# A retention layer and a feed-forward layer in one kernel: two small products swapped, the scores of two chunks in one place, one more block by seven products

## The chip, the cores and the metric

The kernel runs on one core of a Trainium2 chip. The metric is the device time of one execution in microseconds (us); the median of three executions is given. The kernel is written in Bass with its own instruction order: the order in which the Python code issues an operation is the order in which its engine runs it (`tc.manual_schedule()`), and each engine waits, in that order, for the semaphores of what it reads and of the buffers that it overwrites.

## The reference

```python
gamma = 1.0 - 2.0 ** (-5.0 - np.arange(H))            # H = 8 heads
for t in range(S):                                    # S = 768 tokens, 4 sequences
    state = gamma * state + outer(k[t], v[t])         # 64 x 64 for each head
    y[t] = scale * q[t] @ state
x = y, heads side by side                             # 3072 tokens x 512
h = x @ w_in                                          # 512 -> 2048
g = h * tanh(log1p(exp(h)))                           # mish
out = g @ w_out                                       # 2048 -> 512, float32
```

## The kernel before

**Chunks and blocks.** The 3072 tokens are 24 chunks of 128, six to a sequence. `BLOCKS` puts them into 11 blocks: block 0 of four chunks, blocks 1 to 10 of two chunks (256 tokens). For each chunk the recurrence is done by products: `scores` (8 products of 64 rows by 128 columns, one for each head, into a PSUM tile `at`), `mask` (VectorE multiplies them with a triangle, giving `am`), `outer` (key by value into `u_ps`), `state` (VectorE adds the last state into `su`, then `su` times the decay gives `st`, on VectorE or, in the blocks by seven products, on GpSimd), and `y_two` (`past` from the state, `present` from `am`), whose result ScalarE copies out as `xt`. All this is done one block ahead: while block b goes through the feed-forward layer, the scores, masks and y of block b+1 lie between its matmuls. GpSimd casts and scales q, k and v (`casts`, three operations a chunk), and SyncE's queue turns them by a transposing DMA (`next_chunk`).

**Plain blocks.** A block of 256 tokens has 64 matmuls of 256 columns for the first product (`g1`, L475), a mish on ScalarE after each eight, and 32 matmuls of 512 columns for the second (`g2_mm`, L497). Its other work is placed by `plan_of`, a table from step to work.

**Blocks by seven products.** From block `SEVEN` on, `g1_seven` and `seven` use the scheme of Strassen and Winograd: a product of 2 by 2 blocks from seven products of half the size, not eight. In `g1_seven` the hidden features are four slices of 512; slices 0 and 2 are made together by seven products of 8 matmuls with 128 columns (L599), slices 1 and 3 are plain (`plain`, L623: 8 matmuls of 256 columns each, two for a slice). In `seven` the whole second product is made by seven products of 8 matmuls with 256 columns (L688). The operands are sums of blocks:
- `wsum` (`win_sums`) and `tmat` (`weight_sums`) are sums of the weights, made once, on VectorE;
- `xsum` (`x_sums`) and `gsum` (`sums_a` for s1 and s2 in two halves, `sums_b` for s3, `sums_c` for s4) are sums of a block's x and g, made for each block, on VectorE.

Three PSUM tiles `pb`, `px`, `pe` accumulate several products; between two of them the running value is copied out (`snap`, ScalarE: `m1`, `m5`, `u2`) and added later on VectorE (`plus`, giving `c11`, `c12`, `c22`). So a product that goes on accumulating in `px` waits until the copy or the sum that reads `px` is done. `mish_of` then makes g from each quarter. Half 0 of `gsum`'s s2 reads g of slices 0 and 2, half 1 reads slices 1 and 3, thus the mish of `plain(3, 1)`, the last of the first product. The second product begins with a(0,0), a(0,1), then s2 with t2: its matmuls 0 to 3 read half 0, matmuls 4 to 7 half 1.

**Where the other work lies in such a block.** `steps_of` is a table from a place's name to work: `p2` (outer, first state), `p6`, `p7` (second state, `sums_a` half 0), `p4` (first chunk's scores and mask), `end` (`sums_a` half 1, second chunk's scores, the next casts), and in `seven` `m2` (second mask), `m7` (`y_two`), `m3` (`x_sums`).

**The weight sums.** `win_sums` runs in block 1 (`blk + 2 == SEVEN`), `weight_sums` in block 2 (`blk + 1 == SEVEN`), one item after each step of the block's loop. Their tiles come from pools that they share with the staging buffers of the weights (`wt`) and the g tiles of block 0 (`g0`).

Of the kernel before, what the change touches and what calls it, by code (L numbers as in the profile page):

```python
# [9 lines left out]
FP16 = mybir.dt.float16  # L10
FP32 = mybir.dt.float32
AF = mybir.ActivationFunctionType
ALU = mybir.AluOpType
# [3 lines left out]
def kernel(  # L17
# [12 lines left out]
    P = 128  # L30
# [4 lines left out]
    TB = 512  # L35
# [5 lines left out]
    NFB = d_ff // P  # L41
    NBP = d_model // P
# [22 lines left out]
    wstage = ctx.enter_context(tc.tile_pool(name="rn_wstage", bufs=3))  # L65
    gp = ctx.enter_context(tc.tile_pool(name="rn_g", bufs=2))
# [29 lines left out]
    for c in range(2):  # L96
        t = tri_first[c * HB:(c + 1) * HB]
# [17 lines left out]
    gtiles, tmats, gsums = {}, [], []  # L115
    wsums, hsnaps, tsums = [], [], {}
    nsnap = [0]
    SEVEN = 3
    nload, ncast = [0], [0]
    stores = []  # L120

# [389 lines left out]
    def weight_sums(half):  # L511
        n, hf = NFB // 2, d_model // 2
        if half == 0:
            tmats.extend(
                wstage.tile([P, 2, n, hf], FP16, name="tmat", tag="wt", bufs=4)
                for _ in range(2))
            gsums.extend(
                wstage.tile([P, 4, n, P], FP16, name="gsum", tag="wt", bufs=4)
                for _ in range(2))
        f = slice(half * FPS, (half + 1) * FPS)  # L520
        t1, t2 = tmats[0][:, 0, f], tmats[0][:, 1, f]
        t3, t4 = tmats[1][:, 0, f], tmats[1][:, 1, f]
        b11, b12 = wouts[half][:, :, :hf], wouts[half][:, :, hf:]
        b21, b22 = wouts[half + 2][:, :, :hf], wouts[half + 2][:, :, hf:]
        sub = ALU.subtract
        return [
            lambda: nc.vector.tensor_tensor(t1, b12, b11, op=sub),
            lambda: nc.vector.tensor_tensor(t2, b22, t1, op=sub),
            lambda: nc.vector.tensor_tensor(t3, b22, b12, op=sub),
            lambda: nc.vector.tensor_tensor(t4, b21, t2, op=sub),  # L530
        ]
# [12 lines left out]
        nc.vector.tensor_tensor(s2, s1, a11, op=ALU.subtract)  # L544

    def win_sums():
        wsums.append(gp.tile([P, 4, NBP // 2, TB], FP16, name="wsum", tag="g0"))
        hsnaps.append(gp.tile([P, 4, TB], FP32, name="hsnap", tag="g0"))
        sub, n = ALU.subtract, NBP // 2
        todo = []  # L550
        for half in range(2):
            s1, s2, s3, s4 = [
                wsums[0][:, i, :, half * (TB // 2):(half + 1) * (TB // 2)] for i in range(4)]
            a11, a12 = wins[0, half][:, :n], wins[0, half][:, n:]
            a21, a22 = wins[2, half][:, :n], wins[2, half][:, n:]
            todo.append([(s1, a21, a22, ALU.add), (s2, s1, a11, sub)])
            todo.append([(s3, a11, a21, sub), (s4, a12, s2, sub)])

        def work(ops):
            for dst, x, y, f in ops:  # L560
                nc.vector.tensor_tensor(dst, x, y, op=f)
        return [lambda ops=ops: work(ops) for ops in todo]
# [14 lines left out]
    def g1_seven(blk, steps):  # L577
        n = NBP // 2
        gt = gtiles[blk, 0] = gp.tile([P, NFB, 2 * P], FP16, name="g", tag="g")
        for fb in range(NFB):  # L580
            gts[blk, fb] = gt[:, fb]
        pb, px, pe = [mmps.tile([P, FPS, P], FP32, name="h_ps", tag="mm") for _ in range(3)]

        def a(i, j):
            return lambda f, d: win(2 * i, f, j * n + d)

        def s(i):
            return lambda f, d: wsums[0][:, i - 1, d, f * P:(f + 1) * P]

        def b(i, j):  # L590
            return lambda d: x_part(blk, i, j)[:, d]

        def t(i):
            return lambda d: tsums[blk][:, i - 1, d]

        def mm(h_ps, w, x, first=False):
            for f in range(FPS):
                for d in range(n):
                    nc.tensor.matmul(  # L599
                        h_ps[:, f], w(f, d), x(d), start=first and f == 0 and d == 0,  # L600
                        stop=d == n - 1, skip_group_check=True)

        def snap(h_ps):
            x = hsnaps[0][:, nsnap[0] % 4].rearrange("p (f t) -> p f t", t=P)
            nsnap[0] += 1
            nc.scalar.copy(x, h_ps)  # L606
            return x

        def mish_of(i, j, h):
            nc.scalar.activation(  # L610
                gt[:, 2 * i * FPS:(2 * i + 1) * FPS, j * P:(j + 1) * P], h, AF.Mish,
                scale=inv_boost3)

        def plus(h_ps, x):
            h = hp.tile([P, FPS, P], FP32, name="hsum", tag="hsum", bufs=3)
            nc.vector.tensor_tensor(h, h_ps, x, op=ALU.add)  # L616
            return h

        def plain(s, half):
            h_ps = mmps.tile([P, 2, 2 * P], FP32, name="h_ps", tag="mm")  # L620
            for j in range(2):
                for bp in range(NBP):
                    nc.tensor.matmul(  # L623
                        h_ps[:, j], win(s, 2 * half + j, bp), xt(blk, bp),
                        start=bp == 0, stop=bp == NBP - 1)
            fb = s * FPS + 2 * half
            nc.scalar.activation(gt[:, fb:fb + 2], h_ps, AF.Mish, scale=inv_boost3)  # L627

        def step(name):
            for fn, *args in steps.get(name, ()):  # L630
                fn(*args)

        mm(px, a(0, 0), b(0, 0), True)
        m1 = snap(px)
        mm(pb, a(0, 1), b(1, 0), True)
        c11 = plus(pb, m1)
        step("p2")
        mm(pe, s(1), t(1), True)
        m5 = snap(pe)
        mm(px, s(2), t(2))  # L640
        u2 = snap(px)
        mish_of(0, 0, c11)
        step("p6")
        plain(1, 0)
        mm(pe, s(4), b(1, 1))
        c12 = plus(pe, u2)
        mm(px, s(3), t(3))
        c22 = plus(px, m5)
        mish_of(0, 1, c12)
        mish_of(1, 1, c22)  # L650
        step("p7")
        plain(1, 1)
        mm(px, a(1, 1), t(4))
        mish_of(1, 0, px)
        step("p4")
        plain(3, 0)
        plain(3, 1)
        step("end")

# [104 lines left out]
    def first_block():  # L764
# [85 lines left out]
            31: [(y_two, 1)],  # L850
        }
        o_tiles = [None] * CPB
        for u in range(2, 2 * NFB):
            if u < NFB:
                g1(0, u)
            elif u < 2 * NFB - 2:
                w = u - NFB
                for t in range(CPB):
                    if w == 0:
                        o_tiles[t] = mmps.tile([P, d_model], FP32, name="o_ps", tag="mm")  # L860
                    g2_mm(o_tiles[t], 0, t, w)
            else:
                for t in range(CPB // 2) if u % 2 == 0 else range(CPB // 2, CPB):
                    for w in range(NFB - 2, NFB):
                        g2_mm(o_tiles[t], 0, t, w)
                    g2_out(o_tiles[t], 0, t, 1)
            for fn, *args in plan.get(u + 1, ()):
                fn(*args)

    def next_chunk(g):  # L870
        if g < NCK:
# [15 lines left out]
    def steps_of(blk):  # L887
        a, nb = first[blk] + 4, blk + 1
        ahead = nb < len(BLOCKS)

        def only(*work):
            return list(work) if ahead else []
        return {
            "p2": only((outer_next, nb), (state_next, nb, 0)),
            "p6": [(cast_to, a + 1), (next_chunk, a), (store_due, 1)],
            "p7": [(store_due, 2), *only((state_next, nb, 1)), (sums_a, blk, 0)],
            "p4": [(store_due, 3), *only((scores, a - 2), (mask, a - 2))],
            "end": [(sums_a, blk, 1), *only((scores, a - 1)),
                    (cast_to, a + 2), (next_chunk, a + 1)],
            "m2": only((mask, a - 1)),  # L900
            "m7": only((y_two, nb)),
            "m3": only((x_sums, nb)),
        }

    def plan_of(blk):
        a = first[blk] + 4
        early, then_seven = blk == 1, blk + 1 == SEVEN
        plan = {1: [(cast_to, a + 1)],
# [8 lines left out]
    for blk in range(1, len(BLOCKS)):  # L917
        if blk >= SEVEN:
            steps = steps_of(blk)
# [5 lines left out]
        extra = []  # L925
        if blk + 1 == SEVEN:
            extra = weight_sums(0) + weight_sums(1)
        if blk + 2 == SEVEN:
            extra = win_sums()
        for u in range(2 * n1):  # L930
            store_due(u)
            if u < n1:
# [1 line left out]
            else:  # L934
                t, part = divmod(u - n1, 4)
# [8 lines left out]
            if extra:  # L944
                extra.pop(0)()
        if blk + 1 == SEVEN:
            x_sums(SEVEN)
    store_due(2 * NFB)
# [30 lines left out]
```

## Time and profile before

| | |
|---|---|
| time, median of 3 (lowest to highest) | 208.18 us (207.81 to 208.47) |
| the profiled execution's own time | 207.9 us |
| its span in the profile | 206.0 us |
| TensorE (PE) busy | 197.2 us |
| VectorE (DVE) busy | 143.1 us |
| ScalarE (ACT) busy | 98.3 us |
| GpSimd (POOL) busy | 90.6 us |
| granted TensorE clock | 1.0 over the span |

The start of each block is the start of its first matmul in the timeline of PE: block 1 at 50.12 us, block 2 at 66.31, block 3 at 82.43, then 97.80, 113.03, 128.49, 143.73, 158.97, 174.43, and block 10 at 189.67. The length of a block is the difference of two such starts. The work of a block depends a little on where a sequence of six chunks begins: of blocks 3 to 9, blocks 5 and 8 have 8 outer and 8 past products, blocks 4 and 7 have 8 and 4, blocks 3, 6 and 9 have 4 and 8; block 2 has 8 and 8, and block 10 has none, and no scores.

A row of the timeline reads: start, time from its first start to its last end, engine, line, operation, output and input, number of instructions, and in brackets the idle time before it with what ended it. A matmul's time in such a row holds its way through the array (219 ns for 128 columns, 273 ns for 256), so the time that a matmul takes of PE is read from the distance of the starts: eight matmuls of 128 columns take 0.45 us, eight of 256 columns 0.87 us.

### The profile page before, as it was taken

What the parts mean: (1) busy time and instruction counts of PE and PEld (TensorE: products, weight loads), DVE (VectorE), ACT (ScalarE), POOL (GpSimd) and SP (SyncE); (2) the same over time, 40 slices, a digit from 0 to 9 for tenths busy, and PEclk for the clock granted to TensorE, in tenths of its full rate; (3) what the DMA queues carried; (4) which work ended last, traced back from release to release, by engine and by line L of the source; (5) the groups of instructions that cost most, each with busy time, mean ns of one, the idle gap of its engine ahead of it and who ended that gap; (6) DMA issues with size and microseconds to landing.
All of it is one profiled execution on the core that took longest, in us unless ns stands there. A gap on an engine that the chain in (4) does not pass through costs nothing.

```text
span 206.0 us, 5180 instructions
## 1 busy us (share of the span) xinstructions
PE 197.2 (96%) x2167; PEld 150.2 (73%) x2167; DVE 143.1 (69%) x234; ACT 98.3 (48%) x171; POOL 90.6 (44%) x83
## 2 busy tenths in 40 slices
PE   6788999999999999999999999999999999999993
PEld 2355444456855865988988988888888888888882
DVE  2796644169937986788897787686897687686542
ACT  2462763242611621653653653753753743843840
POOL 4162000519955760399182594598091693200000
PEclk9999999999999999999999999999999999999999
DMA  5999999998999999939998159959999062200202
GB/s 177 299 316 363 386 387 279 292 220 176 201 247 262 216 221 237 180 70 214 227 253 178 35 109 225 178 105 267 194 256 190 18 156 56 100 0 26 80 28 77
DMA packets 95896, 38.64 MB, mean 188 GB/s; under 512 B 82305, under 2 KB 89985, under 8 KB 95873
## 3 DMA queue, kind: packets, MB, share of 16 engines
q1 hardware_dynamic: 92608, 37.50, 80.3%
q10 hardware_dynamic: 3264, 0.82, 2.4%
q8 instruction: 17, 0.28, 0.5%
q14 instruction: 7, 0.05, 0.1%
HBM read 27.30 MB, written 6.29 MB: 163 GB/s over the span
## 4 chain that ended last, share of the span: by engine, by line
PE 83%; DVE 9%; ACT 2%; DMA 2%; issue 2%; DVEq 0%
PE o_ps L688 24%; PE h_ps L475 13%; PE o_ps L497 11%; PE h_ps L599 11%; PE h_ps L623 11%; DVE hsum L616 5%; PE at L371 3%; PE y_ps L414 2%; DMA qfirst<-in_q_dram 2%; PE y_ps L404 2%; PE u_ps L385 2%; DVE am L377 1%; PE h_ps L760 1%; ACT xt L460 1%; DVE qfirst L196 1%
## 5 line engine op out<-in xcount | busy, mean ns | idle before, releaser
L319 POOL TENSOR_TENSOR qk<-qf,qvs 128x512 f16<-128x512 f32 x20 | 22.5, 1127 | 28.4 <-DMA qf<-in_q_dram 26.4
L623 PE MATMUL h_ps<-xt,win 128*128 128x256 f16 x256 | 31.9, 273 | 0.0
L398 POOL TENSOR_TENSOR st<-su,gcm 128x512 f16<-128x512 f32 x9 | 11.9, 1321 | 41.7 <-DVE su L397 31.3
L497 PE MATMUL o_ps<-wout,g 128*128 128x512 f16 x128 | 30.1, 380 | 0.0
L324 POOL TENSOR_SCALAR qk<-kf 128x512 f16<-128x512 f32 x18 | 27.8, 1546 | 2.1 <-DMA kf<-in_k_dram 0.6
L377 DVE TENSOR_TENSOR am<-at,tri 128x1024 f16<-128x1024 f32 x20 | 24.1, 1214 | 4.6 <-PE at L371 4.6
L688 PEld LDWEIGHTS <-gsum 128*128 128x128 f16 x256 | 24.4, 98 | 3.6 <-DVE gsum L666 0.2
L475 PE MATMUL h_ps<-xt,win 128*128 128x256 f16 (+1 forms) x184 | 26.5, 305 | 0.3
L623 PEld LDWEIGHTS <-win 128*128 128x128 f16 x256 | 23.7, 98 | 3.1
L475 PEld LDWEIGHTS <-win 128*128 128x128 f16 x184 | 18.0, 98 | 9.0 <-issue 0.8
L491 ACT ACTIVATE g<-h_ps 128x512 f16<-128x512 f32 x32 | 19.0, 597 | 11.4 <-PE h_ps L475 10.0
L325 POOL TENSOR_TENSOR v<-vf,qvs 128x512 f16<-128x512 f32 x20 | 21.6, 1079 | 6.3 <-DMA vf<-in_v_dram 4.9
L460 ACT CAST xt<-y_ps 128x1024 f16<-128x1024 f32 x10 | 10.1, 1012 | 28.9 <-PE y_ps L414 21.6
L616 DVE TENSOR_TENSOR hsum<-h_ps,hsnap 128x512 f32<-128x512 f32 x24 | 15.8, 686 | 9.4 <-PE h_ps L599 8.2
L688 PE MATMUL o_ps<-tmat,gsum 128*128 128x256 f16 x192 | 22.3, 273 | 0.0
L627 ACT ACTIVATE g<-h_ps 128x512 f16<-128x512 f32 x32 | 19.0, 593 | 4.8 <-PE h_ps L623 4.8
L497 PEld LDWEIGHTS <-g 128*128 128x128 f16 x128 | 11.7, 98 | 13.0 <-issue 0.3
L606 ACT COPY hsnap<-h_ps 128x512 f32<-128x512 f32 x24 | 13.3, 588 | 15.6 <-PE h_ps L599 15.6
L688 PEld LDWEIGHTS <-g 128*128 128x128 f16 x192 | 18.2, 98 | 2.8
L694 ACT COPY snap<-o_ps 128x256 f32<-128x256 f32 x24 | 8.9, 372 | 20.3 <-PE o_ps L688 20.3
L702 DVE TENSOR_TENSOR osb<-o_ps,snap 128x256 f32<-128x256 f32 x24 | 10.1, 419 | 11.7 <-PE o_ps L688 9.0
L610 ACT ACTIVATE g<-hsum 128x512 f16<-128x512 f32 x24 | 15.0, 635 | 3.4 <-DVE hsum L616 3.4
(94 smaller groups left out, 291.0 us busy)
## 6 DMA issues: line engine op xcount, KB each, us to landing
kf<-in_k_dram SPq DMA_DIRECT2D x23, 256.0 KB, 5.1
vf<-in_v_dram SPq DMA_DIRECT2D x23, 256.0 KB, 5.1
out_dram<-osb SPq DMA_DIRECT2D x22, 256.0 KB, 3.8
qf<-in_q_dram SPq DMA_DIRECT2D x19, 256.0 KB, 4.0
wt<-in_moe_w_out_dram SPq DMA_DIRECT2D x3, 1024.0 KB, 8.9
wi<-in_moe_w_in_dram SPq DMA_DIRECT2D x4, 512.0 KB, 7.3
wi<-in_moe_w_in_dram SPq DMA_DIRECT2D x2, 1024.0 KB, 11.3
qfirst<-in_q_dram SPq DMA_DIRECT2D x2, 512.0 KB, 5.0
```

The source lines that it names most:

```text
L319: nc.gpsimd.tensor_tensor(q16, qf, qs.unsqueeze(2).broadcast_to((P, H, D)), op=ALU.mult)
L324: nc.gpsimd.tensor_scalar(k16, kf, BOOST, None, op0=ALU.mult)
L325: nc.gpsimd.tensor_tensor(v16, vf, vs.unsqueeze(2).broadcast_to((P, H, D)), op=ALU.mult)
L377: nc.vector.tensor_tensor(am, ats.pop(g), tri.unsqueeze(1).unsqueeze(1).broadcast_to((P, 2, HP, C)), op=ALU.mult)
L475: nc.tensor.matmul(h_ps[:, j], win(s, f, bp), xt(blk, bp), start=(bp == 0), stop=(bp == NBP - 1))
L491: nc.scalar.activation(gt, h_ps, AF.Mish, scale=inv_boost3)
L497: nc.tensor.matmul(o_ps, gts[blk, fb][:, t * P:(t + 1) * P], wouts[s][:, f, cols], start=(fb == 0), stop=(fb == NFB - 1))
L599: nc.tensor.matmul(h_ps[:, f], w(f, d), x(d), start=first and f == 0 and d == 0, stop=d == n - 1, skip_group_check=True)
L616: nc.vector.tensor_tensor(h, h_ps, x, op=ALU.add)
L623: nc.tensor.matmul(h_ps[:, j], win(s, 2 * half + j, bp), xt(blk, bp), start=bp == 0, stop=bp == NBP - 1)
L627: nc.scalar.activation(gt[:, fb:fb + 2], h_ps, AF.Mish, scale=inv_boost3)
L688: nc.tensor.matmul(o_ps, x(f), w(f), start=first and f == 0, stop=f == n - 1, skip_group_check=True)
```

## The change

It makes block 2 a block by seven products too (`SEVEN = 2`): `weight_sums` moves from block 2 to block 1, and `win_sums` from block 1 into the second product of block 0, in eight items of one operation each. For that `wsum` and one of the two `gsum` tiles change pools. In `g1_seven`, s3 with t3 (into `px`) and its sum `c22` come ahead of s4 with b(1,1) (into `pe`) and its sum `c12`, and their two mish activations change places with them. The scores of both chunks and the first mask lie in a new place `h2`, between `plain(3, 0)` and `plain(3, 1)`; the second mask stays at `m2`.

```diff
-    SEVEN = 3
+    SEVEN = 2
...
-            gsums.extend(
-                wstage.tile([P, 4, n, P], FP16, name="gsum", tag="wt", bufs=4)
-                for _ in range(2))
+            gsums.append(wstage.tile([P, 4, n, P], FP16, name="gsum", tag="wt", bufs=4))
+            gsums.append(gp.tile([P, 4, n, P], FP16, name="gsum", tag="g0"))
+            hsnaps.append(gp.tile([P, 4, TB], FP32, name="hsnap", tag="g0"))
...
     def win_sums():
-        wsums.append(gp.tile([P, 4, NBP // 2, TB], FP16, name="wsum", tag="g0"))
-        hsnaps.append(gp.tile([P, 4, TB], FP32, name="hsnap", tag="g0"))
+        wsums.append(wstage.tile([P, 4, NBP // 2, TB], FP16, name="wsum", tag="wt", bufs=4))
...
-            todo.append([(s1, a21, a22, ALU.add), (s2, s1, a11, sub)])
-            todo.append([(s3, a11, a21, sub), (s4, a12, s2, sub)])
+            todo.append([(s1, a21, a22, ALU.add)])
+            todo.append([(s2, s1, a11, sub)])
+            todo.append([(s3, a11, a21, sub)])
+            todo.append([(s4, a12, s2, sub)])
...
         plain(1, 0)
+        mm(px, s(3), t(3))
+        c22 = plus(px, m5)
         mm(pe, s(4), b(1, 1))
         c12 = plus(pe, u2)
-        mm(px, s(3), t(3))
-        c22 = plus(px, m5)
+        mish_of(1, 1, c22)
         mish_of(0, 1, c12)
-        mish_of(1, 1, c22)
         step("p7")
         plain(1, 1)
         mm(px, a(1, 1), t(4))
         mish_of(1, 0, px)
         step("p4")
         plain(3, 0)
+        step("h2")
         plain(3, 1)
         step("end")
...
+        extra = []
         for u in range(2, 2 * NFB):
...
+            if u == NFB + 1:
+                extra = win_sums()
+            if extra:
+                extra.pop(0)()
...
-            "p4": [(store_due, 3), *only((scores, a - 2), (mask, a - 2))],
-            "end": [(sums_a, blk, 1), *only((scores, a - 1)),
-                    (cast_to, a + 2), (next_chunk, a + 1)],
+            "p4": [(store_due, 3)],
+            "h2": only((scores, a - 2), (scores, a - 1), (mask, a - 2)),
+            "end": [(sums_a, blk, 1), (cast_to, a + 2), (next_chunk, a + 1)],
...
-        if blk + 2 == SEVEN:
-            extra = win_sums()
```

## The prediction, made before the changed kernel ran

> **What bounds the kernel now.** First the page: engines, then the chain of waits.
>
> ```profile
> PE 197.2 (96%) x2167; PEld 150.2 (73%) x2167; DVE 143.1 (69%) x234; ACT 98.3 (48%) x171; POOL 90.6 (44%) x83
> PE 83%; DVE 9%; ACT 2%; DMA 2%; issue 2%; DVEq 0%
> ```
>
> PE is busy 197.2 of 206.0 us and holds 83% of the chain; the granted clock is 1.0. So what counts is PE's own work and the places where it stands still. For these, PE's timeline of block 4 (97.80 to 113.03), from `plain(1, 0)` to s2 with t2:
>
> ```profile
> 100.03 1.04 PE L623 MATMUL h_ps<-xt,win 128*128 128x256 f16 x8
> 100.90 0.61 PE L599 MATMUL h_ps<-xt,wsum 128*128 128x128 f16 x8
> 101.35 0.61 PE L599 MATMUL h_ps<-xsum,wsum 128*128 128x128 f16 x8
> 101.80 1.04 PE L623 MATMUL h_ps<-xt,win 128*128 128x256 f16 x8
> 102.96 0.61 PE L599 MATMUL h_ps<-xsum,win 128*128 128x128 f16 x8
> 103.50 0.40 PE L371 MATMUL at<-qkt 64*128 64x128 f16 x8
> 103.83 1.92 PE L623 MATMUL h_ps<-xt,win 128*128 128x256 f16 x16
> 105.68 0.40 PE L371 MATMUL at<-qkt 64*128 64x128 f16 x8
> 106.01 1.92 PE L688 MATMUL o_ps<-wout,g 128*128 128x256 f16 x16
> 107.77 2.78 PE L688 MATMUL o_ps<-tmat,gsum 128*128 128x256 f16 x24
> ```
>
> `plain(1, 1)` starts at 101.80 and takes 0.87, to 102.67. The next product, a(1,1) with t4, starts at 102.96: 0.29 us lost. It goes on in `px`, so it waits for `c22`, the second of the two sums in the first row below (from VectorE's timeline; the row after it is ScalarE's, the copies `m5` and `u2`):
>
> ```profile
> 101.62 1.29 DVE L616 TENSOR_TENSOR hsum<-h_ps,hsnap 128x512 f32<-128x512 f32 x2 [0.76 <-PE h_ps L599]
> ...
> 99.84 1.07 ACT L606 COPY hsnap<-h_ps 128x512 f32<-128x512 f32 x2 [0.81 <-PE h_ps L599]
> ```
>
> The sums end at 102.91, and PE goes on 0.05 later. The same wait stands in all eight blocks by seven products.
>
> Second, the scores. The 8 at 103.50 move what follows by more than their row says: from 102.96 to 103.83 are 0.87, of which the product takes 0.45, so 0.42 to 0.43 for the scores; likewise 105.68 (103.83 to 106.01 less 16 x 0.109 = 0.44). In plain block 2 both chunks' scores stand together:
>
> ```profile
> 66.31 7.15 PE L475 MATMUL h_ps<-xt,win 128*128 128x256 f16 x64
> 73.39 0.62 PE L371 MATMUL at<-qkt 64*128 64x128 f16 x16
> 73.95 2.76 PE L497 MATMUL o_ps<-wout,g 128*128 128x512 f16 x12
> ```
>
> 73.95 - 66.31 - 64 x 0.109 = 0.66 us for 16, against 0.87 for twice 8: 0.21 less.
>
> **The change, part by part.**
>
> *The swap.* s3 with t3 now ends 0.45 earlier and `c22` is the first sum. Counted from the block's start in block 4: s3 with t3 runs at 3.10 to 3.55, `c22` starts 0.27 behind it (as the first sum does now: 101.35 to 101.62) and ends 0.69 later, at 4.51; with 0.05, PE may go on at 4.56. But PE is busy with s4 and `plain(1, 1)` until 4.87. The wait is gone, covered by 0.3. A smaller one comes in: s3 with t3 accumulates on U2, so it waits for the copy `u2`, ending at 99.84 + 1.07 = 100.91, plus 0.05, where PE is ready at 100.90. So 0.06 stays. Behind it on PE is all the rest, so it counts in full; the sums and mish behind it move by 0.06 too. Gain 0.29 - 0.06 = 0.23 to 0.24 in each of blocks 3 to 10: 1.9 us.
>
> *The scores in one place.* 0.21 us in each of blocks 3 to 9 (block 10 has none): 1.45 us. The second `at` tile is the one that `u_ps` leaves when the second `su` is done (102.83 + 0.68, at 5.7 in the block; the scores start at 6.2): no wait. The first mask is queued on VectorE between the two halves of `sums_a`; scores end near 6.9 with the way out, and half 0 is done at 6.7 to 7.6 as now, so the mask ends by 8.8, about where it ends now.
>
> *What this uncovers.* `plain(3, 1)` ended at 105.57 (7.77 in the block) and ends at 7.77 again: 0.44 saved ahead of it, 0.43 of scores moved in front of it. The second product now follows at once and not 0.44 later. So s2's matmul 4, the first on half 1 of s2, is due 0.87 + 0.87 + 0.44 = 2.18 behind `plain(3, 1)`, where it had 2.6. Half 1 needs the mish of `plain(3, 1)` (L543 starts 0.84 behind its end) and two operations of VectorE; undisturbed (0.46 + 0.42) they are done at 1.72, disturbed not:
>
> ```profile
> 121.65 0.49 DVE L543 TENSOR_TENSOR gsum<-g 128x512 f16<-128x512 f16 x1 [0.79 <-ACT g L627]
> 122.17 1.15 DVE L544 TENSOR_TENSOR gsum<-gsum,g 128x512 f16<-128x512 f16 x1
> ...
> 182.83 0.42 DVE L543 TENSOR_TENSOR gsum<-g 128x512 f16<-128x512 f16 x1 [0.80 <-ACT g L627]
> 183.29 0.42 DVE L544 TENSOR_TENSOR gsum<-gsum,g 128x512 f16<-128x512 f16 x1
> ...
> 120.59 1.27 POOL L398 TENSOR_TENSOR st<-su,gcm 128x512 f16<-128x512 f32 x1
> 121.82 1.22 POOL L319 TENSOR_TENSOR qk<-qf,qvs 128x512 f16<-128x512 f32 x1
> ```
>
> In block 5 L544 takes 1.15 where it takes 0.42 in block 9: GpSimd's L319 began at 121.82 and ended at 123.04, L544 at 123.32. GpSimd's order in a block hangs on the first `su`, which the change leaves at its place, so the collision should come again at the same place. End of half 1 behind `plain(3, 1)`, from the two timelines: 2.51 us in blocks 3, 5 and 8 (92.52, 123.32, 169.27), 2.19 in 4 and 7, 2.08 and 1.73 in 6 and 9. With 0.05 for the signal against 2.18: 0.38 given back in blocks 5 and 8, 0.1 in 4 and 7 (0.06 each from the later sums), nothing in 6 and 9. Block 3 stands in its sequence as block 6 does and was late only as the first block by seven (its `su` at 84.77, 2.34 behind the start, against 1.88 in block 6): nothing there, and its length falls from 15.37 to block 6's 15.24, 0.13 gained. In all 0.95 back.
>
> The Trainium skill (SBUF — State Buffer, "Who interferes with whom") says that a VectorE operation with two SBUF inputs and a GpSimd operation that reads SBUF lock each other out, the first to start holding the port to its end. The rows above agree for L319; but block 5's L544 of half 0 (119.30, 0.43 us) lay in GpSimd's scaling of k (118.03 to 119.52) undelayed. Held to the letter the rule speaks against this change: an earlier s2 meets more locks. That is the rival "all collide" below.
>
> *Block 2.* Plain it takes 82.43 - 66.31 = 16.12. Block 8, with the same small work, takes 15.46; less 0.24 and 0.21, 15.01 without a wait at s2. As the first block by seven its `x_sums` come behind the last output copy of block 1 (66.22), so the first `su`, the state on GpSimd and all casts run some 0.5 late, as in block 3 now. GpSimd's second state then falls on 7.8 to 9.1, where half 1 begins (8.6): I take L543 to 9.4, then L319, L544 ending near 10.7, due 9.95: 0.8. Length 15.8, gain 0.3; bounds 0 and 1.1.
>
> *The weight sums.* Eight wsum operations (0.41 undisturbed, up to 1.26 beside GpSimd in block 1) follow the last wout cast at 35.68; six lie ahead of the copy L362 at 40.45, which PE waits for: 6 x 0.41 = 2.5 to 4.3 in a gap of 4.78. The other two fit into gaps of 0.5 and 1.05. Nothing on the path; bounds 0 and 0.6. The eight tmat operations took 7.3 together in block 2 (1.45 at most each); in block 1, from 50.80, they end at 58.1 to 59.3, and the masks start at 60.23: nothing. GpSimd's casts of chunks 8 and 9 may slip a few tenths; the turn of chunk 9 lands at 65.78 + 5.2 = 71.0, its scores come at 72.6. On SP `next_chunk` of chunks 10 and 11 falls behind the two states on GpSimd, to about 74 and 79 from 73.11 and 78.52; they are needed at 88. The seam of blocks 1 and 2 (PE waits 0.3 for `xt`) stays.
>
> **Sum.** 1.9 + 1.45 + 0.13 + 0.3 - 0.95 = 2.8 us: 207.9 to 205.1 for a profiled execution, and, as that one lies 0.3 under the median, 208.18 to 205.35 for the median, given as 205.3.
>
> **The rivals.**
> 1. *Fewer collisions.* GpSimd and VectorE fall apart by some tenths and s2 never waits: 1.9 + 1.45 + 0.13 + 1.1 = 4.6, 203.6. For: blocks 6 and 9. Against: both engines hang on the same sums.
> 2. *The waits only move.* Either the copy `u2` holds s3 with t3 as long as `c22` held `px`, so the swap doesn't do what it says: the 1.9 are gone, s2 gives back only some 0.3, and 1.45 + 0.13 + 0.3 - 0.3 = 1.6 is left, 206.6. Or s2 gives back 0.3 on average in blocks 3 to 9, 2.1 for 0.95: 1.7 left, 206.5; at its far end all of the 0.44, and block 2 its 0.3: 0.24 + 0.13 left, 207.8, no change. For: 2.51 in three of seven blocks, and `u2` already ends level with PE.
> 3. *All collide, slower.* Place: L543 and L544 of half 1, blocks 2 to 9. The longest of each on record, 0.93 and 1.37, put half 1 at 0.84 + 2.3 = 3.1 to 3.2 behind `plain(3, 1)`, 1.05 late, 8.4 us for eight blocks against 4.6 won: 212.0. It decides from 4.6 / 8 = 0.58 a block. Against it: no block had both at once, and the last has 1.73.
>
> **Chances and range.** A measurement of this kernel tells about 0.3%, 0.6 us. Forecast (204.5 to 206.1) 0.5; rival 1 0.17; rival 2 0.25, of which 0.06 its far end; rival 3 0.08. Faster 0.5 + 0.17 + 0.19 = 0.86, same 0.06, slower 0.08. The range takes in rival 1, and rival 2 without its far end: 203.5 to 207.0.
>
> **What would show it.** PE's timeline: no gap ahead of a(1,1) with t4, at most 0.1 ahead of s3 with t3; 16 scores in one row, 0.66 in all; blocks 4, 6, 7 and 9 at 14.8 to 14.9 us, blocks 5 and 8 at 15.4, block 10 0.24 shorter, block 2 at 15.8. VectorE's: L544 of half 1 at 10.3 in blocks 5 and 8. Wrong, if half 1 ends later than 2.6 behind `plain(3, 1)` in most blocks, or if blocks 0 and 1 lengthen.

## The result, and the profile after

The changed kernel takes 205.52 us (median of 4 runs, 205.25 to 205.62), beside 208.0 us for the kernel before (median of 4, 207.78 to 208.47): 0.9876 of the time, with a 95% interval of 0.9854 to 0.9897. It is faster, by 2.5 us or 1.2%. The profiled execution took 205.6 us, with a span of 203.8 us and a granted clock of 1.0. The page's rows of engines and of the chain by engine:

```profile
PE 195.1 (96%) x2215; PEld 152.5 (75%) x2215; DVE 146.9 (72%) x247; ACT 99.8 (49%) x177; POOL 93.9 (46%) x85
PE 85%; DVE 7%; ACT 3%; DMA 2%; issue 1%; DVEq 0%
```

PE is busy 2.1 us less than before, and its share of the chain rises from 83 to 85% while VectorE's falls from 9 to 7%. PE's timeline of block 4 (97.34 to 112.27), the stretch that answers to the one shown of before:

```profile
99.57 1.04 PE L624 MATMUL h_ps<-xt,win 128*128 128x256 f16 x8
100.51 0.61 PE L600 MATMUL h_ps<-xsum,wsum 128*128 128x128 f16 x8
100.95 0.61 PE L600 MATMUL h_ps<-xt,wsum 128*128 128x128 f16 x8
101.40 1.04 PE L624 MATMUL h_ps<-xt,win 128*128 128x256 f16 x8
102.27 0.61 PE L600 MATMUL h_ps<-xsum,win 128*128 128x128 f16 x8
102.72 1.04 PE L624 MATMUL h_ps<-xt,win 128*128 128x256 f16 x8
103.69 0.62 PE L371 MATMUL at<-qkt 64*128 64x128 f16 x16
104.24 1.05 PE L624 MATMUL h_ps<-xt,win 128*128 128x256 f16 x8
105.12 1.91 PE L690 MATMUL o_ps<-wout,g 128*128 128x256 f16 x16
106.87 2.92 PE L690 MATMUL o_ps<-tmat,gsum 128*128 128x256 f16 x24
```

Three things are to be seen. `plain(1, 1)` (101.40) is followed by a(1,1) with t4 at 102.27, 0.87 later, its own length: the 0.29 us of before are gone. In its place s3 with t3 starts at 100.51, 0.94 behind the start of `plain(1, 0)` instead of 0.87: 0.07 is left. And the scores stand in one row of 16: the stretch from 102.72 to 105.12 is 2.40 us, less 16 matmuls of 0.109 there are 0.66 for the scores, as in the plain block of before.

What these two places hang on, from VectorE's and ScalarE's timelines: the sums `c22` and `c12`, and the copies `m5` and `u2`.

```profile
101.22 1.29 DVE L617 TENSOR_TENSOR hsum<-h_ps,hsnap 128x512 f32<-128x512 f32 x2 [1.33 <-PE h_ps L600]
...
99.38 1.07 ACT L607 COPY hsnap<-h_ps 128x512 f32<-128x512 f32 x2 [0.81 <-PE h_ps L600]
```

The copies end at 100.45, and s3 with t3 goes on at 100.51. The sums still end late, at 102.51, but `px` now waits for the first of them alone.

The last row of PE's fence is 2.92 long where 2.78 is undisturbed: s2 has begun to wait. In blocks 2 and 5 it is seen as a split row:

```profile
76.44 0.60 PE L690 MATMUL o_ps<-tmat,gsum 128*128 128x256 f16 x4
77.49 2.36 PE L690 MATMUL o_ps<-tmat,gsum 128*128 128x256 f16 x20 [0.44 <-DVE gsum L544]
...
121.80 0.60 PE L690 MATMUL o_ps<-tmat,gsum 128*128 128x256 f16 x4
122.66 2.36 PE L690 MATMUL o_ps<-tmat,gsum 128*128 128x256 f16 x20 [0.27 <-DVE gsum L544]
```

Four matmuls take 4 x 0.109 = 0.44, so the fifth was due at 76.88 and 122.24: 0.61 lost in block 2, 0.42 in block 5 (0.43 in block 8). What is late is L544 of half 1; here are VectorE and GpSimd in block 5:

```profile
120.88 0.55 DVE L543 TENSOR_TENSOR gsum<-g 128x512 f16<-128x512 f16 x1 [0.60 <-ACT g L628]
121.46 1.15 DVE L544 TENSOR_TENSOR gsum<-gsum,g 128x512 f16<-128x512 f16 x1
...
119.88 1.26 POOL L398 TENSOR_TENSOR st<-su,gcm 128x512 f16<-128x512 f32 x1
121.11 1.22 POOL L319 TENSOR_TENSOR qk<-qf,qvs 128x512 f16<-128x512 f32 x1
```

L544 takes 1.15, and ends at 122.61, 0.28 behind L319's end (122.33): the same collision as before, which now has someone waiting for it.

Lengths of the blocks, from the start of the first product's matmuls on PE to that of the next block (block 10: to the start of the last product of its second product); these are worked out from PE's timelines of each kernel. "Sum" is the whole row.

| kernel | 1 | 2 | 3 | 4 | 5 | 6 | 7 | 8 | 9 | 10 | sum |
|---|---|---|---|---|---|---|---|---|---|---|---|
| before | 16.19 | 16.12 | 15.37 | 15.23 | 15.46 | 15.24 | 15.24 | 15.46 | 15.24 | 12.15 | 151.70 |
| after | 16.19 | 15.58 | 14.79 | 14.93 | 15.45 | 14.80 | 14.92 | 15.46 | 14.79 | 11.92 | 148.83 |

That is 2.87 us from blocks 1 to 10. The spans differ by 2.2 only, because block 0's plain first product (L475) began at 20.61 before and at 21.27 after: 0.66 us, ahead of the first instruction that the change moves. Another execution of the same changed kernel (below) has it at 20.18, so this delay does not belong to the change. The medians (2.5) lie between.

### The profile page after: what moved, and what is told of

It reads as the page before. It is cut to its first block, busy times and chain, and to the rows that moved or that the text cites. A ratio compares the mean times of both kernels' runs of the same rounds, so it can differ in the third digit from the quotient of the medians.

```text
span 203.8 us, 5296 instructions
## 1 busy us (share of the span) xinstructions
PE 195.1 (96%) x2215; PEld 152.5 (75%) x2215; DVE 146.9 (72%) x247; ACT 99.8 (49%) x177; POOL 93.9 (46%) x85
## 4 chain that ended last, share of the span: by engine, by line
PE 85%; DVE 7%; ACT 3%; DMA 2%; issue 1%; DVEq 0%
PE o_ps L690 25%; PE h_ps L624 16%; PE h_ps L600 14%; PE h_ps L475 9%; PE o_ps L497 8%; PE at L371 3%; PE y_ps L414 3%; DMA qfirst<-in_q_dram 2%; PE y_ps L404 2%; DVE gsum L544 2%; PE u_ps L385 2%; DVE am L377 1%; PE h_ps L762 1%; ACT xt L460 1%; DVE gsum L543 1%
## 5 line engine op out<-in xcount | busy, mean ns | idle before, releaser
L624 PE MATMUL h_ps<-xt,win 128*128 128x256 f16 x288 | 37.3, 273 | 0.0
L319 POOL TENSOR_TENSOR qk<-qf,qvs 128x512 f16<-128x512 f32 x20 | 23.4, 1172 | 23.3 <-DMA qf<-in_q_dram 23.3
L398 POOL TENSOR_TENSOR st<-su,gcm 128x512 f16<-128x512 f32 x11 | 14.4, 1307 | 42.3 <-DVE su L397 42.3
L690 PEld LDWEIGHTS <-gsum 128*128 128x128 f16 x288 | 27.0, 98 | 6.1 <-DVE gsum L544 2.3
L624 PEld LDWEIGHTS <-win 128*128 128x128 f16 x288 | 26.4, 98 | 3.3
L690 PE MATMUL o_ps<-tmat,gsum 128*128 128x256 f16 x216 | 25.8, 273 | 1.0 <-DVE gsum L544 1.0
L617 DVE TENSOR_TENSOR hsum<-h_ps,hsnap 128x512 f32<-128x512 f32 x27 | 17.8, 687 | 12.4 <-PE h_ps L600 10.7
L628 ACT ACTIVATE g<-h_ps 128x512 f16<-128x512 f32 x36 | 21.4, 593 | 5.6 <-PE h_ps L624 5.5
L690 PEld LDWEIGHTS <-g 128*128 128x128 f16 x216 | 21.1, 98 | 2.5
L497 PE MATMUL o_ps<-wout,g 128*128 128x512 f16 x96 | 22.7, 380 | 0.0
L475 PE MATMUL h_ps<-xt,win 128*128 128x256 f16 (+1 forms) x120 | 19.4, 322 | 0.1
L491 ACT ACTIVATE g<-h_ps 128x512 f16<-128x512 f32 x24 | 14.2, 597 | 8.4 <-PE h_ps L475 6.9
L600 PEld LDWEIGHTS <-wsum 128*128 128x128 f16 x288 | 17.2, 98 | 0.7
L475 PEld LDWEIGHTS <-win 128*128 128x128 f16 x120 | 11.7, 97 | 7.8 <-issue 0.4
```

The costliest lines, as they stand in the source:

```text
L319: nc.gpsimd.tensor_tensor(q16, qf, qs.unsqueeze(2).broadcast_to((P, H, D)), op=ALU.mult)
L475: nc.tensor.matmul(h_ps[:, j], win(s, f, bp), xt(blk, bp), start=(bp == 0), stop=(bp == NBP - 1))
L497: nc.tensor.matmul(o_ps, gts[blk, fb][:, t * P:(t + 1) * P], wouts[s][:, f, cols], start=(fb == 0), stop=(fb == NFB - 1))
L600: nc.tensor.matmul(h_ps[:, f], w(f, d), x(d), start=first and f == 0 and d == 0, stop=d == n - 1, skip_group_check=True)
L624: nc.tensor.matmul(h_ps[:, j], win(s, 2 * half + j, bp), xt(blk, bp), start=bp == 0, stop=bp == NBP - 1)
L690: nc.tensor.matmul(o_ps, x(f), w(f), start=first and f == 0, stop=f == n - 1, skip_group_check=True)
```

## The experiments

The first four share runs of the kernel before of 207.53 us (207.28 to 207.91), the other four, on another chip, of 207.36 us (207.26 to 207.93). `sum` is that of the table above, where before has 151.70.

| run | us | ratio to before, 95% | sum |
|---|---|---|---|
| the swap alone | 206.38 | 0.9943 (0.9930 to 0.9956) | 150.39 |
| the scores alone | 207.91 | 1.0015 (1.0006 to 1.0024) | 151.75 |
| the third block alone | 206.71 | 0.9961 (0.9948 to 0.9973) | 151.05 |
| after, k first for three chunks | 203.43 | 0.9799 (0.9786 to 0.9813) | 147.68 |
| after, again | 204.62 | 0.9862 (0.9848 to 0.9876) | 149.04 |
| after, k first for all chunks | 209.62 | 1.0098 (1.0082 to 1.0114) | 153.46 |
| scores alone, k first for three | 206.46 | 0.9949 (0.9935 to 0.9963) | 150.55 |
| before, k first for three | 207.49 | 1.0001 (0.9991 to 1.0011) | 151.76 |

**The theory and its rivals.** The theory: the swap takes PE's gap away, the merging takes half of the scores' fixed cost away, and part of this comes back at s2, because half 1's sums collide with GpSimd's scaling of q (L319). Rival A: the loss at s2 is not the collision but the chain PE, mish, sums itself, so no order on GpSimd would help. Rival B: the parts are independent, and each alone brings its share.

**The swap alone.** Kernel before, with one hunk:

```diff
         plain(1, 0)
+        mm(px, s(3), t(3))
+        c22 = plus(px, m5)
         mm(pe, s(4), b(1, 1))
         c12 = plus(pe, u2)
-        mm(px, s(3), t(3))
-        c22 = plus(px, m5)
+        mish_of(1, 1, c22)
         mish_of(0, 1, c12)
-        mish_of(1, 1, c22)
```

> The kernel before with the swap alone (s3 with t3 and c22 ahead of s4 with b(1,1) and c12, their mish swapped too). Theory (the wait of px for c22 is removed, 0.23 to 0.24 us in each of eight blocks, and s2 gives back some 0.2 in blocks 5 and 8): 1.9 - 0.4 = 1.5 us less than before, about 206.5; blocks 4, 6, 7 and 9 at 15.0 us, blocks 5 and 8 at 15.4, a gap of 0.06 ahead of s3 with t3, none ahead of a(1,1) with t4. Rival (the wait only moves to the copy u2): within 0.3 us of before, with a gap of 0.2 to 0.3 ahead of s3 with t3.

Measured: 0.9943, 1.15 us less, where 1.5 was expected. Blocks 3, 4, 6, 7 and 9 are 15.21, 15.00, 15.01, 15.00 and 15.00, 0.16 to 0.24 shorter, and block 10 is 11.92, 0.23 shorter. Blocks 5 and 8 are 15.47, where 15.4 was expected: nothing won. Block 5 (from 112.21) on PE, VectorE and GpSimd:

```profile
121.96 3.02 PE L688 MATMUL o_ps<-tmat,gsum 128*128 128x256 f16 x24
...
120.60 0.78 DVE L543 TENSOR_TENSOR gsum<-g 128x512 f16<-128x512 f16 x1 [0.50 <-ACT g L627]
121.41 1.15 DVE L544 TENSOR_TENSOR gsum<-gsum,g 128x512 f16<-128x512 f16 x1
...
121.05 1.23 POOL L319 TENSOR_TENSOR qk<-qf,qvs 128x512 f16<-128x512 f32 x1
```

PE's row is 3.02 instead of 2.78: the 0.24 that the swap wins is waited off whole in the same block. L544 ends at 122.56, 0.28 behind L319's end, at the same place in the block as ever: the end of half 1 is set by GpSimd there, not by PE.

**The scores alone.** Kernel before, with `step("h2")` between `plain(3, 0)` and `plain(3, 1)`, and the steps:

```diff
-            "p4": [(store_due, 3), *only((scores, a - 2), (mask, a - 2))],
-            "end": [(sums_a, blk, 1), *only((scores, a - 1)),
-                    (cast_to, a + 2), (next_chunk, a + 1)],
+            "p4": [(store_due, 3)],
+            "h2": only((scores, a - 2), (scores, a - 1), (mask, a - 2)),
+            "end": [(sums_a, blk, 1), (cast_to, a + 2), (next_chunk, a + 1)],
```

> The kernel before with the two scores and the first mask in the new place alone. Theory (16 scores together take 0.66 where twice 8 take 0.87, but s2 comes due 0.4 earlier behind plain(3,1) and waits where VectorE and GpSimd collide): 0.2 less in each of blocks 3, 4, 6, 7 and 9, about nothing in 5 and 8: 1.0 us less than before, 207.0, with a wait of 0.2 to 0.5 ahead of s2's matmul 4 in blocks 5 and 8. Rival (no collision at s2, the place alone counts): 7 x 0.21 = 1.5 less. Rival (all blocks give it back): no change.

Measured: 1.0015, 0.3 us more, where 1.0 less was expected; the expectation failed. Blocks 4, 6, 7 and 9 are 15.03, the 0.21 shorter that was expected. But blocks 5 and 8 are 15.98 and 15.97, 0.52 longer than before. Block 5 (from 112.18):

```profile
121.94 0.60 PE L689 MATMUL o_ps<-tmat,gsum 128*128 128x256 f16 x4
123.10 2.36 PE L689 MATMUL o_ps<-tmat,gsum 128*128 128x256 f16 x20 [0.56 <-DVE gsum L544]
...
121.03 1.27 DVE L543 TENSOR_TENSOR gsum<-g 128x512 f16<-128x512 f16 x1 [0.60 <-ACT g L627]
122.33 0.71 DVE L544 TENSOR_TENSOR gsum<-gsum,g 128x512 f16<-128x512 f16 x1
...
119.74 1.27 POOL L398 TENSOR_TENSOR st<-su,gcm 128x512 f16<-128x512 f32 x1
120.97 1.04 POOL L319 TENSOR_TENSOR qk<-qf,qvs 128x512 f16<-128x512 f32 x1
```

Here L319 started 0.06 ahead of L543, and L543 was held to 122.30, 0.29 behind L319's end. In the changed kernel L543 starts 0.23 ahead of L319, while the state update L398 still runs. L543 needs 0.55, not 0.42, and ends 0.29 behind L398's end (121.43 and 121.14); then L319 takes 1.22 instead of 1.04, and only L544 is held by L319. Counted from the block's start, half 1 ends at 10.86 with the scores alone and at 10.34 with the whole change (122.61 less 112.27); s2's fifth matmul was due at 10.20 and 9.97. So a lead of some tenths on VectorE decides whether one operation of half 1 or both are held, and that is 0.52 us a block. Where L543 arrives, and where L319 starts, in block 5 of four kernels, each read off the timelines and counted from the block's start:

| | before | swap alone | scores alone | after |
|---|---|---|---|---|
| L543 | 8.62 | 8.39 | 8.85 | 8.61 |
| L319 | 8.79 | 8.84 | 8.79 | 8.84 |
| s2 waits | 0 | 0.24 | 0.72 | 0.42 |

The merging puts 16 scores ahead of `plain(3, 1)` instead of 8 and so L543 0.23 later; the swap puts it 0.23 earlier. The two parts are not independent (rival B falls): together L543 stands where it stood before.

**The third block alone.** Kernel before, with `SEVEN = 2` and the moved weight sums, without the other two parts.

> Block 2 by seven products and the weight sums in blocks 0 and 1, product order and scores as before. Theory: block 2 falls from 16.12 us to 15.46 plus 0.1, block 3 from 15.37 to 15.24, blocks 0 and 1 keep their lengths: 0.7 us less than before, about 207.3. Rival (the sums in blocks 0 and 1 hold up the copies and masks that PE waits for): blocks 0 and 1 longer by 0.3 to 0.7, and no gain. The first matmul of block 0's plain first product (L475) tells the head apart: it started at 20.61 us in the profile of before and at 21.27 in that of after; if the change of the instruction stream causes this, it is at 21.2 to 21.3 here and at 20.6 in the kernels whose head and length are those of before; if it is chance, it varies without this order.

Measured: 0.9961, 0.82 us less, where 0.7 was expected. Block 2 is 15.58 instead of 16.12, block 3 is 15.24 instead of 15.37, and the sum is 0.65 less; block 1 is as long as before (16.20). Block 0's plain first product starts at 20.21, so the later start in the first execution of the changed kernel does not come from the moved weight sums.

Alone the three parts are worth -1.31, +0.05 and -0.65 in the sums, -1.91, and -2.87 together. The other 0.96 us lie in blocks 5 and 8 (1.06, by the waits at s2: 2 x 0.24 and 2 x 0.72 in the two first runs, 0.85 with all parts together) and in block 3 (0.13), less 0.25 in blocks 4 and 7, which wait only with all parts together. Block 2 has its 15.58 here already: half 1 ends at 10.46 us into it (76.37 less 65.91), as in the changed kernel (77.43 less 66.97), both times behind L319. There the swap and the merging bring nothing, and what they save is waited off at s2.

**k first for three chunks.** The changed kernel, with GpSimd scaling k ahead of q for chunks 11, 17 and 23, those whose scaling meets half 1 in blocks 2, 5 and 8. k's operation has one tensor input, q's has two:

```diff
+        k_first = g > CPB + 2 and g % NCH == NCH - 1
+        if k_first:
+            nc.gpsimd.tensor_scalar(k16, kf, BOOST, None, op0=ALU.mult)
         nc.gpsimd.tensor_tensor(
             q16, qf, qs.unsqueeze(2).broadcast_to((P, H, D)), op=ALU.mult)
...
-        else:
+        elif not k_first:
```

> The changed kernel, where GpSimd scales k ahead of q for the last chunk of each sequence (chunks 11, 17, 23), so that in blocks 2, 5 and 8 the operation with two SBUF inputs that ran beside L543 and L544 of half 1 is replaced by one with a single SBUF input. Theory (L544 is held up by GpSimd's L319, which has two SBUF inputs, and PE waits for L544): L544 of half 1 takes 0.42 instead of 1.15 us in these three blocks, the waits ahead of s2's matmul 4 (0.62, 0.43 and 0.43 us) are gone or below 0.1, 1.3 us less than the changed kernel, about 204.2, and faster than both. Rival (any GpSimd operation that reads SBUF holds L544): L544 still takes 1 us or more, no change against the changed kernel. Rival (PE waits for something else behind it, such as s4's sum): L544 is short and the time the same.

Measured: 203.43 us, 0.9799; the changed kernel alone was 0.9876 and, on another chip, 0.9862. The sum is 1.15 less than in the changed kernel, where 1.3 was expected. Blocks 2, 5 and 8 fall from 15.58, 15.45 and 15.46 to 15.28, 15.03 and 15.02; no other block moves by more than 0.02. Block 5 (from 110.92; here L545 and L546 are L543 and L544, L320 is k, L321 is q):

```profile
120.45 2.79 PE L692 MATMUL o_ps<-tmat,gsum 128*128 128x256 f16 x24
...
119.54 0.55 DVE L545 TENSOR_TENSOR gsum<-g 128x512 f16<-128x512 f16 x1 [0.60 <-ACT g L630]
120.12 0.72 DVE L546 TENSOR_TENSOR gsum<-gsum,g 128x512 f16<-128x512 f16 x1
...
118.54 1.26 POOL L400 TENSOR_TENSOR st<-su,gcm 128x512 f16<-128x512 f32 x1
119.88 1.55 POOL L320 TENSOR_SCALAR qk<-kf 128x512 f16<-128x512 f32 x1
121.51 1.04 POOL L321 TENSOR_TENSOR qk<-qf,qvs 128x512 f16<-128x512 f32 x1
```

L546 takes 0.72 beside the scaling of k, not the 1.15 beside that of q, and s2 goes through in one row of 2.79. The expected 0.42 was not reached: k's scaling holds it too, but less. Rival A falls: the sums and the chain of half 1 are the same, only GpSimd's order differs. Block 2 keeps 0.3 of its loss, at another place: its scores waited for the turn of chunk 9, a transposing DMA that landed 6.8 us after its issue in this execution and 5.2 in those of before and after. So blocks 5 and 8 are the clean test.

**The changed kernel again.** No edit, to have it on the chip of the next three.

> The changed kernel once more, beside the kernels of this call on one chip. If the 0.66 us by which its head (up to block 0's plain first product, 21.27 against 20.61 us) was longer belong to the instruction stream, it shows 21.2 again, and its gain stays at 2.2 to 2.5 us; if they were chance, the head is at 20.1 to 20.7, and the gain is that of blocks 1 to 10 in the trace, 2.8 to 2.9.

Measured: 204.62 us, 0.9862, within the first interval: 2.74 us less than before, where 2.8 to 2.9 was expected without the late start. Blocks 5 and 8 are 15.46 again; block 0's plain first product starts at 20.18 where the first execution had 21.27. Block 6 is 14.99 where the first execution had 14.80. There the sum for s4 met GpSimd's next scaling of q and took 1.56 instead of 0.68, so the same kernel can meet one collision more in one execution than in another.

**k first for all chunks.** The same edit with `k_first = g >= CPB + 2`.

> The changed kernel with k scaled ahead of q for every chunk that GpSimd casts (from 6 on). Theory (VectorE's gsum operations and GpSimd's operations with two SBUF inputs shut each other out, the first to start wins, so only the place of each counts): blocks 5 and 8 keep their gain, but in blocks 3 and 6 the scaling of q and v now falls on half 0 of the sums (L543 at 5.6 in the block) and pushes mask and half 1 behind: 0.6 to 1.5 us longer each; blocks 4 and 7 about 0.3 longer: 1 to 2.5 us slower than the changed kernel, 206 to 208. Rival (k first is better as such): as fast as with the order changed for chunks 11, 17, 23 alone, about 203.5.

Measured: 209.62 us, 1.0098, slower than before, and 5.0 us slower than the changed kernel, where 1 to 2.5 was expected. From the waits of PE (engine, line, waited for: us in total, times, longest us), where the changed kernel has 1.0 in 3 times:

```profile
PE o_ps L692 <- DVE gsum L546: 3.6, 7, 1.0
```

With k first, q and v stand back to back, two operations with two inputs each. In blocks 2, 3, 5, 6 and 8 both now fall on half 0 of the sums. VectorE and GpSimd at half 0 of block 5 (114.23 to 129.63; L327 is v), and behind them the second operation of half 1 in block 3 (81.96 to 98.10):

```profile
120.09 1.02 DVE L545 TENSOR_TENSOR gsum<-g 128x512 f16<-128x512 f16 x1
121.15 1.15 DVE L546 TENSOR_TENSOR gsum<-gsum,g 128x512 f16<-128x512 f16 x1
...
119.79 1.04 POOL L321 TENSOR_TENSOR qk<-qf,qvs 128x512 f16<-128x512 f32 x1
120.79 1.22 POOL L327 TENSOR_TENSOR v<-vf,qvs 128x512 f16<-128x512 f32 x1
...
91.53 1.25 DVE L546 TENSOR_TENSOR gsum<-gsum,g 128x512 f16<-128x512 f16 x1
...
91.45 1.04 POOL L321 TENSOR_TENSOR qk<-qf,qvs 128x512 f16<-128x512 f32 x1
```

Half 0 ends late and pushes the mask and half 1 behind it, as was expected for blocks 3 and 6. What was not expected is that half 1's second sum then meets the next chunk's q, in blocks 3, 4, 6 and 7. Blocks 3, 4 and 6 are 16.14, 16.13 and 16.15, 1.2 to 1.35 longer than in the changed kernel, and block 7 is 15.77, 0.85 longer (0.3 was expected for 4 and 7). Blocks 5 and 8, which were to keep their gain, are 15.40.

In block 3 half 1 ends some 3.3 us behind `plain(3, 1)`, a little later than the prediction's rival 3 had put it (3.1 to 3.2). So a loss of that size a block is real in this kernel, though by another way than rival 3 described: it is half 0 and one operation of half 1 that are held, not both of half 1. What keeps the changed kernel from it is where q, k and v happen to fall.

**Two controls.** The merging alone, and the kernel before, each with k first for the three chunks.

> The kernel before with the scores in one place alone, which was 0.3 us slower than before, now with k scaled ahead of q for chunks 11, 17 and 23. Theory (the scores' 0.21 a block are real and were eaten in blocks 5 and 8, at 15.97, by the lock that let GpSimd's L319 in ahead of L543): blocks 5 and 8 fall to 15.25, the others stay at 15.03: 7 x 0.21 = 1.45 us less than before. Rival (the scores in one place cost elsewhere): no faster than before by more than 0.5.

> The kernel before with k scaled ahead of q for chunks 11, 17 and 23 alone. Theory (in the kernel before s2 came due late enough, so this order hides under the wait for c22 and the later start of the second product): no change within 0.2 us; blocks 5 and 8 at 15.4 to 15.5. Rival (this order is a gain of its own, whatever the change does): 0.8 to 1.2 us less than before.

Measured: 0.9949 with the merging alone, where it had 1.0015; blocks 5 and 8 fall from 15.98 and 15.97 to 15.25, and blocks 3 to 9 together by 1.41 against before, where 1.45 was expected. The time is only 0.9 less, in part because block 2 is 16.37 instead of 16.12: its scores waited for a transposing DMA that landed 6.4 us after its issue. Half 1 and the scaling of k in block 5:

```profile
121.87 0.43 DVE L545 TENSOR_TENSOR gsum<-g 128x512 f16<-128x512 f16 x1 [0.60 <-ACT g L629]
122.33 0.71 DVE L546 TENSOR_TENSOR gsum<-gsum,g 128x512 f16<-128x512 f16 x1
...
121.94 1.71 POOL L320 TENSOR_SCALAR qk<-kf 128x512 f16<-128x512 f32 x1
```

The merging's 0.21 a block is there once the collision is out of the way. In the kernel before the same order is worth nothing: 1.0001 (0.9991 to 1.0011), blocks 5 and 8 still 15.46 and 15.47. That settles the theory's last step: before, the collision is there but half 1 isn't awaited; it costs time only since the change draws s2 forward. Blocks 5 and 8 are 0.22 to 0.24 longer than their neighbours in all kernels without a wait too, so that part is their own work.

## Why the prediction was right, point by point

**The sum.** 2.83 us were forecast for blocks 1 to 10, 2.87 are there; 205.3 against 205.52 in the median. That the sums agree to 0.04 is in part luck: block 2 wins 0.24 more than forecast, and s2 gives back 0.16 more.

**The swap.** Right: the gap of 0.29 goes, and 0.07 comes at `u2`, where 0.06 was forecast; block 10 is 0.23 shorter. So rival 2's first form (`u2` holds s3 as long as `c22` held `px`) is out.

**The scores.** Right in size: 0.66 for 16. What the prediction had not seen is the part's danger: alone it wins nothing (1.0015), since L543 then comes behind L319. The swap, forecast as 0.24 a block on its own, also pays for that.

**What is uncovered at s2.** The step is right as a mechanism, shown by the runs with k first, and nearly right in size. Blocks 5 and 8 were to give back 0.38 and gave 0.42 and 0.43; 4 and 7 0.1, and they are 14.93 and 14.92 beside 14.79 and 14.80, 0.13; 3, 6 and 9 nothing, as it is. In all 1.11 for 0.95, in good part because L544 ends at 10.34 in block 5, where 2.51 behind `plain(3, 1)` gave 10.28. Rival 1 (no wait at all, 4.6 us less than before) asked the engines to fall apart by themselves; put apart by hand in three chunks they give 4.1 less (207.53 to 203.43), with 0.3 still lost in block 2 and 0.13 each in blocks 4 and 7.

**Block 2.** Mis-sized: 15.8 forecast, 15.58 measured. The wait at s2 is 0.61 where 0.8 was taken, and the rest of the block is 14.97 where 15.01 was taken. The gain is 0.54, not 0.3. The way there is as forecast (the state from 7.72 to 8.99 in the block, L543 to 9.28, then L319), but L544 ends at 10.46, not near 10.7.

**The port.** The prediction set the Trainium skill's rule aside for the scaling of k, because half 0's L544 lay beside it undelayed. That is right only well behind that operation's start. The trace of before has the other case too, in block 4's half 1 (L543 at 106.49 took 0.82, with k begun at 106.42), and the changed kernel has it again:

```profile
106.10 0.82 DVE L543 TENSOR_TENSOR gsum<-g 128x512 f16<-128x512 f16 x1
...
106.03 1.49 POOL L324 TENSOR_SCALAR qk<-kf 128x512 f16<-128x512 f32 x1
```

This is part of what makes half 1 late in blocks 4 and 7. Over all ten traces, L543 and L544 take 0.81 or 0.82 when they begin 0.07 or 0.08 us behind the start of k's scaling, 0.67 to 0.74 at 0.15 to 0.40 behind, and 0.41 to 0.43 from 0.60 behind on.

The Trainium skill (SBUF — State Buffer, "Who interferes with whom") says that the first to start holds the shared port for the whole instruction and that the order of issue decides who is blocked. The second half of this agrees with the trace: 0.06 behind L319 L543 takes 1.27, and 0.23 ahead of it 0.55, while L319 itself becomes longer. The first half agrees nearly for operations with two inputs on GpSimd, not for its scaling of k, beside which L546 ran from 120.12 to 120.84, well inside 119.88 to 121.43. Whether it is the one input or the kind of operation that makes the scaling of k milder, no run tells apart: all of GpSimd's operations with two inputs here are TENSOR_TENSOR, and the scaling of k is its only TENSOR_SCALAR beside these sums.

**The weight sums.** Right: blocks 0 and 1 are as long as before (29.51 and 16.19). VectorE's rows, the last wsum ahead of the copy that PE waits for, and the last tmat ahead of the masks:

```profile
39.55 0.42 DVE L562 TENSOR_TENSOR wsum<-wsum,win 128x512 f16<-128x512 f16 x1
41.11 0.69 DVE L362 COPY qkt<-t_ps 128x1024 f16<-128x1024 f16 x1 [1.14 <-PE t_ps L360]
...
58.56 1.53 DVE L530 TENSOR_TENSOR tmat<-wout,tmat 128x1024 f16<-128x1024 f16 x1
60.89 2.36 DVE L377 TENSOR_TENSOR am<-at,tri 128x1024 f16<-128x1024 f32 x2 [0.80 <-PE at L371]
```

The first end at 39.97 and leave 1.14; the second at 60.09, 8.6 behind their start at 51.46, where 7.3 to 8.5 was forecast, and leave 0.80. VectorE waits for PE in both places.

## What to carry to other kernels

When a change takes idle time out of the bounding engine, every later wait has that much less slack: list for each operand when it is ready and when it is due after the change, and look for operations that were late all along without being awaited. Where two engines lock each other out, a part's worth hangs on which of two operations starts first, so parts measured alone need not add up; here -1.31, +0.05 and -0.65 made -2.87. And when such a lock is what remains, try the order of the other engine's work for the few steps concerned: three chunks with k ahead of q make the fastest kernel of this study (203.43 us, 0.9799), while the same order everywhere makes one slower than before.

## What was not expected of the hardware

When GpSimd's two-input operation holds L543 or L544, the held one ends 0.27 to 0.29 us behind that operation's recorded end, in all ten traces, though undisturbed it needs 0.42 by itself; by these figures it is let in some 0.14 ahead of that end. GpSimd's one-input scaling, mostly 1.49 to 1.55 us long, costs them 0.25 to 0.4 us when they begin 0.07 to 0.40 us behind its start, and nothing from 0.60 on. Block 0's plain first product starts at 20.1 to 21.3 us from execution to execution, with the same stream of instructions ahead of it; single profiled spans of this kernel are therefore not to be compared below 1 us. Lengths of blocks mostly repeat to 0.02, with exceptions that a trace explains: 0.19 in block 6 of the changed kernel (one collision more) and 0.25 to 0.3 in block 2 of two runs (a transposing DMA that landed late).
